# Linear attention and MLP on one core: k and v by casting software loads in nine rows per partition, with a block-diagonal k

## The chip, the cores and the metric

The kernel runs on 1 core of one Trainium2 chip. The metric is the device time of one execution in microseconds (us), lower is better. A change counts as faster or slower from 2% on; below that it is "same". TensorE is called PE, its weight load PEld, VectorE DVE, ScalarE ACT, GpSimd POOL, SyncE SP, as in the profile.

## The reference

For each of 8 batches and 8 heads (576 positions, 64 columns each), k and v are contracted over the positions, q is multiplied by the 64 x 64 result, each row is normalized by its root mean square and scaled; all heads side by side are the input of an MLP with a sigmoid gate.

```python
kv  = einsum('bhsd,bhse->bhde', k, v)            # 8 x 8 heads, s = 576, d = e = 64
out = einsum('bhsd,bhde->bhse', q, kv)
x   = out / sqrt(mean(out * out, -1) + 1e-6) * g_norm      # -> 4608 x 512
h   = x @ w_in                                    # 512 x 2048
y   = (h * sigmoid(1.702 * h)) @ w_out            # 2048 x 512
```

## The kernel before

The program has nine MLP stages (t = 0 to 8). While PE does the MLP of batch t, the attention of batch t + 1 is woven in at fixed step numbers: "fo" counts the 16 column blocks of the first MLP half (`units1`), n counts the 64 matmuls of the second (`units2`). Stage 8 does the last 64 rows of all batches together and has no attention.

The parts that the change touches:

```python
def load_batch(b, queue=nc.sync):                 # plain f32 loads, 512 of the 576 positions
    for n in "qkv":
        queue.dma_start(out=t, in_=srcs[n][b, :, 0:SM, :].rearrange("h (p j) d -> p h (j d)", j=J))   # J = 4
        # ... (rest rows of q)
    for n in "kv":                                # the other 64 positions: "rest rows"
        queue.dma_start(out=t, in_=srcs[n][b, :, SM:S, :].rearrange("h p d -> p h d"))

def casts(b):                                     # f32 -> f16: VectorE for q, k, v, GpSimd for the rest rows
    # ... 12 tensor_copy on VectorE, 3 on GpSimd

def kv(self, c):                                  # one head pair
    for j in range(J):
        nc.tensor.matmul(t[:, c, :].rearrange("p (l d) -> p l d", l=2), kh[:, c, j, :],
                         vh[:, 2 * c : 2 * c + 2, j * D : (j + 1) * D], start=(j == 0), stop=False)
    nc.tensor.matmul(t[:, c, :], kr[:, c, :], vr[:, c, :], start=False, stop=True)    # rest rows
    if c == NPAIR - 1:
        self.keep_kv()                            # only the two diagonal 64 x 64 blocks are kept
```

Each kv matmul has both heads of a pair in its 128 weight columns and both heads' v in its 128 moving columns, so half of what it computes (head 0 with head 1) is thrown away. Batch 0 has its own start-up path, and batch 1 (`Second`) a third layout, 96 partitions of six rows.

Of the kernel before, what the change touches and what calls it, by code (L numbers as in the profile page):

```python
# [7 lines left out]
F16 = mybir.dt.float16  # L8
# [8 lines left out]
def kernel(  # L17
# [28 lines left out]
    GROUP = 6  # L46
    assert PE_ * NJ == S and PE_ % 32 == 0

    const = ctx.enter_context(tc.tile_pool(name="const", bufs=1))
# [14 lines left out]
    kvb = [const.tile([P, NPAIR, P], F16, name=f"kvb{i}") for i in range(2)]  # L64
    krem = [const.tile([P, NPAIR, P], F16, name=f"krem{i}") for i in range(2)]
    vrem = [const.tile([P, NPAIR, P], F16, name=f"vrem{i}") for i in range(2)]
    qrem = [const.tile([P, 2, P], F16, name=f"qrem{i}") for i in range(2)]
# [26 lines left out]
    def pack(n, dst, c):  # L94

        nc.vector.tensor_copy(
            out=dst[0:PE_, c * NJ * P : (c + 1) * NJ * P].rearrange(
                "p (j l d) -> p j l d", j=NJ, l=2
            ),
            in_=raw[n][0:PE_, c, :].rearrange("p (l j d) -> p j l d", l=2, j=NJ),  # L100
        )


    kh = kbuf[:, 0 : NPAIR * SM].rearrange("p (c j e) -> p c j e", c=NPAIR, j=J)
    qh = qbuf[:, 0 : NPAIR * SM].rearrange("p (c j e) -> p c j e", c=NPAIR, j=J)
    vh = vbuf.rearrange("p c x -> p (c x)")[:, 0 : NPAIR * SM].rearrange("p (h x) -> p h x", h=H)

    def load_batch(b, queue=nc.sync):
        tiles = {}
        for n in "qkv":  # L110
            t = tiles[n] = stage.tile([P, H, J * D], F32, name=f"{n}f", tag=f"{n}f")
            queue.dma_start(
                out=t, in_=srcs[n][b, :, 0:SM, :].rearrange("h (p j) d -> p h (j d)", j=J)
            )
            if n == "q":
                t = tiles["qr"] = stage.tile([P, 4, D], F32, name="qrf", tag="qrf")
                for g in range(2):
                    queue.dma_start(
                        out=t[g * R : (g + 1) * R],
                        in_=q[b, 4 * g : 4 * g + 4, SM:S, :].rearrange("h p d -> p h d"),  # L120
                    )
        for n in "kv":
            t = tiles[n + "r"] = stage.tile([R, H, D], F32, name=f"{n}rf", tag=f"{n}rf")
            queue.dma_start(out=t, in_=srcs[n][b, :, SM:S, :].rearrange("h p d -> p h d"))
        staged[b] = tiles

    def casts(b):
        src = staged[b]
        for n, dst in (("q", qh), ("k", kh), ("v", vh)):
            for c in range(NPAIR):  # L130
                h = slice(2 * c, 2 * c + 2)
                if n == "v":
                    nc.vector.tensor_copy(out=vh[:, h, :], in_=src["v"][:, h, :])  # L133
                else:
                    nc.vector.tensor_copy(
                        out=dst[:, c, :, :].rearrange("p j (l d) -> p j l d", l=2),
                        in_=src[n][:, h, :].rearrange("p l (j d) -> p j l d", j=J),
                    )
        for n, t in (("kr", krem[b % 2][0:R]), ("vr", vrem[b % 2][0:R]), ("qr", qrem[b % 2])):
            nc.gpsimd.tensor_copy(out=t.rearrange("p c (l d) -> p (c l) d", l=2), in_=src[n])  # L140

# [60 lines left out]
    class Attention:  # L202
        ss_pool = (ps_a, "att")

        def __init__(self, b):
# [5 lines left out]
            else:  # L211
                self.x = x.rearrange("p (m r) -> p m r", r=P)
                xT[b] = x.rearrange("p (j c r) -> p c j r", j=J, c=KO)
                self.x16 = attn.tile([P, J, DM], F16, name="x16", tag="x16", bufs=1)

        def kv(self, c):
            if c == 0:
                self.kvp = ps_a.tile([P, NPAIR, P], F32, name="kvp", tag="att")
            t = self.kvp
            for j in range(J):  # L220
                nc.tensor.matmul(  # L221
                    t[:, c, :].rearrange("p (l d) -> p l d", l=2),
                    kh[:, c, j, :],
                    vh[:, 2 * c : 2 * c + 2, j * D : (j + 1) * D],
                    start=(j == 0),
                    stop=False,
                )
            kr, vr = krem[self.b % 2], vrem[self.b % 2]
            nc.tensor.matmul(t[:, c, :], kr[:, c, :], vr[:, c, :], start=False, stop=True)  # L229
            if c == NPAIR - 1:  # L230
                self.keep_kv()

        def keep_kv(self, c0=0, c1=NPAIR):
            for hl in range(2):
                r = slice(hl * D, (hl + 1) * D)
                nc.vector.tensor_copy(self.kb[r, c0:c1, r], self.kvp[r, c0:c1, r])  # L236

# [163 lines left out]
    class Second(Attention):  # L401
# [4 lines left out]
        def pack_q(self, c):  # L406
            pack("q", qbuf, c)

        def pack_k(self, c):
            pack("k", kbuf, c)  # L410

        def kv(self, c):
            if c % 2 == 0:
                self.kvp = ps_a.tile([P, NPAIR, P], F32, name="kvp", tag="att")
            t = self.kvp
            v2 = vbuf[0:PE_, c, :].rearrange("p (l x) -> p l x", l=2)
            for j in range(NJ):
                nc.tensor.matmul(  # L418
                    t[:, c, :].rearrange("p (l d) -> p l d", l=2),
                    kbuf[0:PE_, (c * NJ + j) * P : (c * NJ + j + 1) * P],  # L420
                    v2[:, :, j * D : (j + 1) * D],
                    start=(j == 0),
                    stop=(j == NJ - 1),
                )
            if c % 2:
                self.keep_kv(c - 1, c + 1)

# [201 lines left out]
    for c in (0, 2):  # L629
        early_load("k", 1, c, c + 2)  # L630
        early_load("v", 1, c, c + 2)
        load_w_out(8 + 2 * c, 12 + 2 * c)
    load_batch(2, nc.gpsimd)

# [7 lines left out]
    for t in range(NT):  # L642
# [3 lines left out]
        def at1(i, f, *args):  # L646
            u1.setdefault(i, []).append(lambda: f(*args))
# [7 lines left out]
        if t == 0:  # L655
# [4 lines left out]
            at1(8, start, 1)  # L660
            for r in krem + vrem:
                at1(8, nc.vector.memset, r[R:P], 0.0)
            for c in range(NPAIR):
                at1(12, of(1, "pack_q", c))
                at2(9 + 3 * c, of(1, "q", c))
                at2((21, 21, 33, 33)[c], of(1, "pack_k", c))
                at2((23, 24, 42, 43)[c], of(1, "kv", c))
                o = (27, 31, 48, 52)[c]
                at2(o, of(1, "out", c))
                at2(o + 7 - c // 2, of(1, "ss", c))  # L670
                at2(o + 7 - c // 2, of(1, "apply", c))
        elif b < B:
# [5 lines left out]
            f0 = 5 if t == 1 else 2  # L678
            at1(f0, casts, b)
            at1(f0, start, b)  # L680
            at1(f0, of(b, "transpose_q"))
            if t + 2 < B:
                at1(f0, load_batch, t + 2)
            for c in range(NPAIR):
                at1((10 if t == 1 else 9) + c, of(b, "kv", c))
            at2(6, nc.scalar.preload_act_table_set, "natural_log_exp_and_others")
# [38 lines left out]
```

## Time and profile before

| | before |
|---|---|
| time, median of 3 | 288.6 us (288.12 to 288.72) |
| profiled span | 286.0 us |
| PE busy | 279.8 us, 98% |
| VectorE busy | 110.9 us, 39% |
| a steady stage | 29.90 us, PE busy in all of it |
| DMA busy | 90% or more from 7 to about 57 us, then in bursts |

How to read it: PE is the bound, not only by its busy share but because the chain of work that ended last is PE work end to end. What PE does not execute and does not wait for cannot move the time. The prediction shows the lines.

### The profile page before, as it was taken

Reading aid. Unit: us, or ns where it says so; the run is one execution under the profiler, and the core shown is the slowest. Engines: PE = TensorE matmul, PEld = TensorE weight load, DVE = VectorE, ACT = ScalarE, POOL = GpSimd, SP = SyncE. Lnnn points to the kernel's source line nnn. Section 1 sums busy time; section 2 is a strip of 40 time slices with the busy share of each in tenths; the row PEclk is TensorE's granted clock in tenths of the full one; section 3 lists DMA queues with packets and bytes.
Section 4 is the critical chain, followed back from the end, with each engine's and each line's share of the span. In section 5 each row is a group of like instructions: output and inputs, shape, how many; then the busy total and the mean of one; then the engine's idle time right before and its main releaser. Section 6 shows DMA issues by size and latency. Waiting matters only on the chain.

```text
span 286.0 us, 4103 instructions
## 1 busy us (share of the span) xinstructions
PE 279.8 (98%) x1609; PEld 136.0 (48%) x1609; DVE 110.9 (39%) x219; ACT 156.1 (55%) x273; POOL 49.2 (17%) x66
## 2 busy tenths in 40 slices
PE   7899999999999999999999999999999999999994
PEld 3444544455445544554455445544554444444444
DVE  3530544627651656147603860386227400110001
ACT  2697358766575645574468536763666375017400
POOL 8831430201400140014000500032002100000000
PEclk9999999999999999999999999999999999999999
DMA  8999999999679537893699358954601230011022
GB/s 179 203 206 204 204 255 320 256 250 311 147 178 331 134 75 220 233 271 58 201 205 323 57 183 202 323 92 127 139 2 37 53 133 0 0 73 76 0 73 73
DMA packets 63589, 45.82 MB, mean 160 GB/s; under 512 B 36195, under 2 KB 60515, under 8 KB 62803
## 3 DMA queue, kind: packets, MB, share of 16 engines
q1 hardware_dynamic: 53344, 33.74, 45.4%
q0 software_dynamic: 9504, 10.86, 19.9%
q10 hardware_dynamic: 722, 0.97, 1.2%
q8 instruction: 12, 0.20, 0.3%
q14 instruction: 7, 0.05, 0.1%
HBM read 36.73 MB, written 9.44 MB: 161 GB/s over the span
## 4 chain that ended last, share of the span: by engine, by line
PE 94%; DMA 2%; POOL 2%; issue 0%; DVE 0%; POOLq 0%
PE hT L453 44%; PE o L490 42%; DMA vbuf<-in_v_dram 2%; PE kvp L221 2%; PE outR L287 2%; PE oh L520 1%; PE ss L335 1%; POOL qraw L89 1%; POOL kraw L89 1%; PE outT L255 1%; PE kvp L418 0%; PE kvp L229 0%; POOL vbuf L89 0%; PE q L431 0%; PE outT L266 0%
## 5 line engine op out<-in xcount | busy, mean ns | idle before, releaser
L490 PE MATMUL o<-w_out_sb,gT 128*128 128x512 f16 x560 | 130.7, 379 | 0.0
L462 ACT ACTIVATE gT<-hT 128x512 f16<-128x512 f32 x144 | 84.5, 599 | 77.3 <-PE hT L453 77.2
L453 PE MATMUL hT<-xT,w_in_sb 128*128 128x512 f16 x512 | 116.4, 379 | 0.0
L453 PEld LDWEIGHTS <-w_in_sb 128*128 128x128 f16 x576 | 54.9, 98 | 62.9 <-DMA w_in_sb<-in_moe_w_in_dram 1.6
L490 PEld LDWEIGHTS <-gT 128*128 128x128 f16 x560 | 53.0, 98 | 56.3 <-issue 0.2
L319 POOL TENSOR_TENSOR x<-xr,g_all 128x512 f16<-128x512 f32 x12 | 15.2, 1270 | 141.3 <-DMA vf<-in_v_dram 67.0
L500 DVE COPY osb<-o 128x512 f32<-128x512 f32 x20 | 13.8, 691 | 63.5 <-PE o L490 63.5
L298 DVE TENSOR_REDUCE sum<-sq 128x8 f32<-128x512 f16 x24 | 15.8, 678 | 18.3 <-ACT sq L295 18.3
L236 DVE CAST kvb<-kvp 64x256 f16<-64x256 f32 (+1 forms) x16 | 6.2, 388 | 43.1 <-PE kvp L229 42.0
L312 DVE TENSOR_TENSOR xr<-outR,sum 128x512 f32<-128x512 f32 x24 | 15.5, 686 | 11.1 <-ACT sum L309 11.1
L319 DVE TENSOR_TENSOR x<-xr,g_all 128x512 f16<-128x512 f32 x12 | 15.2, 1267 | 0.7
L295 ACT ACTIVATE sq<-outR 128x512 f16<-128x512 f32 x24 | 13.6, 590 | 2.0 <-PE outR L287 1.6
L275 ACT ACTIVATE sq<-outT 128x512 f16<-128x512 f32 (+1 forms) x16 | 7.7, 482 | 11.9 <-PE outT L255 10.5
L453 PE MATMUL hT<-x_rem,w_in_sb 128*128 128x512 f16 x64 | 14.0, 379 | 0.0
L500 ACT COPY osb<-o 128x512 f32<-128x512 f32 x15 | 8.7, 580 | 6.3 <-PE o L490 6.3
L308 ACT ACTIVATE sum<-sum,eps_t 128x16 f32<-128x16 f32 x12 | 3.7, 308 | 15.0 <-DVE sum L298 14.9
L337 ACT ACTIVATE ln<-ss,eps_t 128x512 f32<-128x512 f32 (+1 forms) x16 | 9.3, 584 | 2.9 <-PE ss L335 2.7
L133 DVE CAST vbuf<-vf 128x512 f16<-128x512 f32 x24 | 9.6, 459 | 2.0 <-DMA vf<-in_v_dram 2.0
L462 ACT ACT_TABLE_LOAD x8 | 10.3, 1283 | 0.1
L221 PEld LDWEIGHTS <-kbuf 128*128 128x128 f16 x96 | 7.4, 98 | 5.7
L287 PEld LDWEIGHTS <-qTd 128*128 128x128 f16 x96 | 7.4, 98 | 5.7
L221 PE MATMUL kvp<-vbuf,kbuf 128*128 128x128 f16 x96 | 9.3, 219 | 0.0
(73 smaller groups left out, 156.8 us busy)
## 6 DMA issues: line engine op xcount, KB each, us to landing
out_dram<-osb SPq DMA_DIRECT2D x6, 1024.0 KB, 4.3
qf<-in_q_dram SPq DMA_DIRECT2D x5, 1024.0 KB, 5.8
kf<-in_k_dram SPq DMA_DIRECT2D x5, 1024.0 KB, 7.8
vf<-in_v_dram SPq DMA_DIRECT2D x5, 1024.0 KB, 10.5
w_out_sb<-in_moe_w_out_dram POOLq DMA_DIRECT2D x4, 512.0 KB, 17.2
out_dram<-osb SPq DMA_DIRECT2D x6, 192.0 KB, 4.2
qf<-in_q_dram POOLq DMA_DIRECT2D x1, 1024.0 KB, 16.7
kf<-in_k_dram POOLq DMA_DIRECT2D x1, 1024.0 KB, 14.8
```

Of the source, the lines that this page charges most:

```text
L133: nc.vector.tensor_copy(out=vh[:, h, :], in_=src["v"][:, h, :])
L221: nc.tensor.matmul(t[:, c, :].rearrange("p (l d) -> p l d", l=2), kh[:, c, j, :], vh[:, 2 * c : 2 * c + 2, j * D : (j + 1) * D], start=(j ...
L287: nc.tensor.matmul(t[:, c * P : (c + 1) * P], self.qT[c][:, j * P : (j + 1) * P], self.kb[:, c, :], start=True, stop=True,)
L295: nc.scalar.activation(sq, t, AFT.Square)
L298: nc.vector.tensor_reduce(out=self.sum2[:, j % 2, :], in_=sq.rearrange("p (h d) -> p h d", h=H), op=ALU.add, axis=mybir.AxisListType.X,)
L312: nc.vector.tensor_mul(xr[:, i], self.o[j + i].rearrange("p (h d) -> p h d", h=H), s2[:, i, :].unsqueeze(2).to_broadcast([P, H, D]),)
L319: (nc.vector if i else nc.gpsimd).tensor_mul(self.x16[:, j + i, :].rearrange("p (h d) -> p h d", h=H), xr[:, i], g_all.unsqueeze(1).to_bro ...
L337: nc.scalar.activation(ln[:, 0:n], t[:, 0:n], AFT.Ln, bias=eps_t, scale=1.0 / D)
L453: nc.tensor.matmul(self.h[fo], w_in_sb[:, ko, fo * P : (fo + 1) * P], self.x[:, ko], start=(ko == 0), stop=(ko == KO - 1),)
L462: nc.scalar.activation(self.gT[:, fo, :], self.h[fo], AFT.Gelu_apprx_sigmoid)
L490: nc.tensor.matmul(os[mo], gT[:, fo, mo * P : (mo + 1) * P], w_out_sb[:, fo, :], start=(fo == 0), stop=(fo == FO - 1),)
L500: copy(osb[:, mo, :], os[mo])
```

## The change

The intent: let the DMA cast k and v on the way in (f32 to f16), so that the f32 staging and the eight casts per batch go; take nine rows per partition in 64 partitions, so that 576 = 64 x 9 comes out even and no rest rows are left; and put the two heads of a pair into the two halves of the partitions. The k of a pair is then made block-diagonal (head 0 in partitions 0 to 63 and columns 0 to 63, head 1 in the rest, zeros elsewhere), so that one matmul of 64 columns does both heads and computes nothing that is thrown away. The same path now serves batch 1.

```diff
-    krem, vrem = ...                                # rest rows
+    kpad = const.tile([P, NPAIR, NH, P], F16)       # block-diagonal k, NH = 9
+    def load_half(n, b, c0, c1):
+        for l in range(2):
+            nc.gpsimd.dma_start(
+                out=raw[n][l * PH : (l + 1) * PH, c0:c1, 0 : NH * D],
+                in_=srcs[n][b].rearrange("(c l) (p j) d -> l p c (j d)", l=2, j=NH)[l][:, c0:c1],
+            )
+        def pack_k(self, c):
+            for l in range(2):
+                r = slice(l * PH, (l + 1) * PH)
+                nc.vector.tensor_copy(
+                    out=kpad[r, c, :, l * D : (l + 1) * D],
+                    in_=kraw[r, c, 0 : NH * D].rearrange("p (j d) -> p j d", j=NH),
+                )
         def kv(self, c):
-            ...                                     # 4 + 1 matmuls of 128 columns
+            for j in range(NH):                     # 9 matmuls of 64 columns
+                nc.tensor.matmul(self.kvp[:, c, :], kpad[:, c, j, :], vbuf[:, c, j * D : (j + 1) * D],
+                                 start=(j == 0), stop=(j == NH - 1))
# ... batch 1, in the second half of stage 0:
-                at2((23, 24, 42, 43)[c], of(1, "kv", c))
-                o = (27, 31, 48, 52)[c]
+                at2((25, 27, 42, 43)[c], of(1, "kv", c))
+                o = (31, 34, 50, 53)[c]
# ... sums and applies of batch 1 at 38, 46, 56, 59 in place of 34, 38, 54, 58
# ... steady stages: k and v of batch t + 2 asked for at fo = 13 (14 in stage 1), after the last kv matmul of batch t + 1
+                at1((10 if t == 1 else 9) + 4, load_kv, t + 2)
```

More of the change, by code (lines that the diff above doesn't have):

```diff
@@ L47 @@
     assert PE_ * NJ == S and PE_ % 32 == 0
+    PH = P // 2
+    NH = S // PH
+    assert PH == D and PH * NH == S
     const = ctx.enter_context(tc.tile_pool(name="const", bufs=1))
@@ L64 @@
     kvb = [const.tile([P, NPAIR, P], F16, name=f"kvb{i}") for i in range(2)]
-    krem = [const.tile([P, NPAIR, P], F16, name=f"krem{i}") for i in range(2)]
-    vrem = [const.tile([P, NPAIR, P], F16, name=f"vrem{i}") for i in range(2)]
+    kpad = const.tile([P, NPAIR, NH, P], F16)
     qrem = [const.tile([P, 2, P], F16, name=f"qrem{i}") for i in range(2)]
@@ L101, in pack @@
         )
-    kh = kbuf[:, 0 : NPAIR * SM].rearrange("p (c j e) -> p c j e", c=NPAIR, j=J)
     qh = qbuf[:, 0 : NPAIR * SM].rearrange("p (c j e) -> p c j e", c=NPAIR, j=J)
-    vh = vbuf.rearrange("p c x -> p (c x)")[:, 0 : NPAIR * SM].rearrange("p (h x) -> p h x", h=H)
-    def load_batch(b, queue=nc.sync):
-        tiles = {}
-        for n in "qkv":
-            t = tiles[n] = stage.tile([P, H, J * D], F32, name=f"{n}f", tag=f"{n}f")
+    def load_half(n, b, c0, c1):
[4 more added lines that the diff above has]
+            )
@@ L112, in load_batch, with load_kv, load_q @@
+    def load_kv(b):
+        load_half("k", b, 0, NPAIR)
+        load_half("v", b, 0, NPAIR)
+    def load_q(b, queue=nc.sync):
+        t = stage.tile([P, H, J * D], F32, name="qf", tag="qf")
+        queue.dma_start(out=t, in_=q[b, :, 0:SM, :].rearrange("h (p j) d -> p h (j d)", j=J))
+        r = stage.tile([P, 4, D], F32, name="qrf", tag="qrf")
+        for g in range(2):
             queue.dma_start(
-                out=t, in_=srcs[n][b, :, 0:SM, :].rearrange("h (p j) d -> p h (j d)", j=J)
-            )
@@ L115, in load_batch @@
-            if n == "q":
-                t = tiles["qr"] = stage.tile([P, 4, D], F32, name="qrf", tag="qrf")
-                for g in range(2):
-                    queue.dma_start(
-                        out=t[g * R : (g + 1) * R],
-                        in_=q[b, 4 * g : 4 * g + 4, SM:S, :].rearrange("h p d -> p h d"),
-                    )
-        for n in "kv":
-            t = tiles[n + "r"] = stage.tile([R, H, D], F32, name=f"{n}rf", tag=f"{n}rf")
-            queue.dma_start(out=t, in_=srcs[n][b, :, SM:S, :].rearrange("h p d -> p h d"))
@@ L125, in load_batch @@
-        staged[b] = tiles
-    def casts(b):
-        src = staged[b]
-        for n, dst in (("q", qh), ("k", kh), ("v", vh)):
-            for c in range(NPAIR):
-                h = slice(2 * c, 2 * c + 2)
-                if n == "v":
-                    nc.vector.tensor_copy(out=vh[:, h, :], in_=src["v"][:, h, :])
-                else:
-                    nc.vector.tensor_copy(
-                        out=dst[:, c, :, :].rearrange("p j (l d) -> p j l d", l=2),
-                        in_=src[n][:, h, :].rearrange("p l (j d) -> p j l d", j=J),
-                    )
-        for n, t in (("kr", krem[b % 2][0:R]), ("vr", vrem[b % 2][0:R]), ("qr", qrem[b % 2])):
-            nc.gpsimd.tensor_copy(out=t.rearrange("p c (l d) -> p (c l) d", l=2), in_=src[n])
+                out=r[g * R : (g + 1) * R],
@@ new lines, in load_q, with cast_q @@
+                in_=q[b, 4 * g : 4 * g + 4, SM:S, :].rearrange("h p d -> p h d"),
+            )
+        staged[b] = (t, r)
+    def cast_q(b):
+        t, r = staged[b]
+        nc.gpsimd.tensor_copy(out=qrem[b % 2].rearrange("p c (l d) -> p (c l) d", l=2), in_=r)
+        for c in range(NPAIR):
+            nc.vector.tensor_copy(
+                out=qh[:, c, :, :].rearrange("p j (l d) -> p j l d", l=2),
+                in_=t[:, 2 * c : 2 * c + 2, :].rearrange("p l (j d) -> p j l d", j=J),
+            )
@@ L214, in __init__ @@
                 self.x16 = attn.tile([P, J, DM], F16, name="x16", tag="x16", bufs=1)
+        def pack_k(self, c):
+            for l in range(2):
+                r = slice(l * PH, (l + 1) * PH)
+                nc.vector.tensor_copy(
+                    out=kpad[r, c, :, l * D : (l + 1) * D],
+                    in_=kraw[r, c, 0 : NH * D].rearrange("p (j d) -> p j d", j=NH),
+                )
         def kv(self, c):
-            if c == 0:
-                self.kvp = ps_a.tile([P, NPAIR, P], F32, name="kvp", tag="att")
-            t = self.kvp
-            for j in range(J):
+            if c % 2 == 0:
+                self.kvp = ps_a.tile([P, NPAIR, D], F32, name="kvp", tag="att")
+            for j in range(NH):
                 nc.tensor.matmul(
-                    t[:, c, :].rearrange("p (l d) -> p l d", l=2),
-                    kh[:, c, j, :],
-                    vh[:, 2 * c : 2 * c + 2, j * D : (j + 1) * D],
+                    self.kvp[:, c, :],
+                    kpad[:, c, j, :],
+                    vbuf[:, c, j * D : (j + 1) * D],
                     start=(j == 0),
-                    stop=False,
+                    stop=(j == NH - 1),
                 )
-            kr, vr = krem[self.b % 2], vrem[self.b % 2]
-            nc.tensor.matmul(t[:, c, :], kr[:, c, :], vr[:, c, :], start=False, stop=True)
-            if c == NPAIR - 1:
-                self.keep_kv()
+            if c % 2:
+                self.keep_kv(c - 1, c + 1)
         def keep_kv(self, c0=0, c1=NPAIR):
@@ L235, in keep_kv @@
                 r = slice(hl * D, (hl + 1) * D)
-                nc.vector.tensor_copy(self.kb[r, c0:c1, r], self.kvp[r, c0:c1, r])
+                nc.vector.tensor_copy(self.kb[r, c0:c1, r], self.kvp[r, c0:c1, :])
         def transpose_q(self):
@@ L407, in pack_q @@
             pack("q", qbuf, c)
-        def pack_k(self, c):
-            pack("k", kbuf, c)
-        def kv(self, c):
-            if c % 2 == 0:
-                self.kvp = ps_a.tile([P, NPAIR, P], F32, name="kvp", tag="att")
-            t = self.kvp
-            v2 = vbuf[0:PE_, c, :].rearrange("p (l x) -> p l x", l=2)
-            for j in range(NJ):
-                nc.tensor.matmul(
-                    t[:, c, :].rearrange("p (l d) -> p l d", l=2),
-                    kbuf[0:PE_, (c * NJ + j) * P : (c * NJ + j + 1) * P],
-                    v2[:, :, j * D : (j + 1) * D],
-                    start=(j == 0),
-                    stop=(j == NJ - 1),
-                )
-            if c % 2:
-                self.keep_kv(c - 1, c + 1)
         def q(self, c):
@@ L629 @@
     for c in (0, 2):
-        early_load("k", 1, c, c + 2)
-        early_load("v", 1, c, c + 2)
+        load_half("k", 1, c, c + 2)
+        load_half("v", 1, c, c + 2)
         load_w_out(8 + 2 * c, 12 + 2 * c)
-    load_batch(2, nc.gpsimd)
+    load_q(2, nc.gpsimd)
     nc.gpsimd.dma_start(out=g_all, in_=g_norm.unsqueeze(0).to_broadcast([P, D]))
@@ L660 @@
             at1(8, start, 1)
-            for r in krem + vrem:
-                at1(8, nc.vector.memset, r[R:P], 0.0)
+            for l in range(2):
+                r = slice(l * PH, (l + 1) * PH)
+                at1(8, nc.vector.memset, kpad[r, :, :, (1 - l) * D : (2 - l) * D], 0.0)
             for c in range(NPAIR):
@@ L666 @@
                 at2((21, 21, 33, 33)[c], of(1, "pack_k", c))
-                at2((23, 24, 42, 43)[c], of(1, "kv", c))
-                o = (27, 31, 48, 52)[c]
+                at2((25, 27, 42, 43)[c], of(1, "kv", c))
+                o = (31, 34, 50, 53)[c]
                 at2(o, of(1, "out", c))
-                at2(o + 7 - c // 2, of(1, "ss", c))
-                at2(o + 7 - c // 2, of(1, "apply", c))
+                if c == NPAIR - 1:
+                    at2(46, load_kv, 2)
+                at2((38, 46, 56, 59)[c], of(1, "ss", c))
+                at2((38, 46, 56, 59)[c], of(1, "apply", c))
         elif b < B:
@@ L678 @@
             f0 = 5 if t == 1 else 2
-            at1(f0, casts, b)
+            at1(f0, cast_q, b)
             at1(f0, start, b)
@@ L682 @@
             if t + 2 < B:
-                at1(f0, load_batch, t + 2)
+                at1(f0, load_q, t + 2)
+                at1((10 if t == 1 else 9) + 4, load_kv, t + 2)
             for c in range(NPAIR):
+                at1(f0, of(b, "pack_k", c))
                 at1((10 if t == 1 else 9) + c, of(b, "kv", c))
```

## The prediction

> **What bounds the kernel now.** I read the page first, for busy time by engine.
>
> ```profile
> PE 279.8 (98%) x1609; PEld 136.0 (48%) x1609; DVE 110.9 (39%) x219; ACT 156.1 (55%) x273; POOL 49.2 (17%) x66
> ```
>
> TensorE (PE) is busy for 98% of the 286.0 us span; VectorE, which the change relieves, for 39%. A busy share is only an average, so I read PE's own waits next, then PE busy time by stretch (columns: stretch, its length, busy time of PE, PEld, DVE, ACT and POOL with instruction counts, granted clock, DMA share, GB/s).
>
> ```profile
> PE idle L569 <- DVE kvb L156: 1.3, 1, 1.3
> PE kv L372 <- DMA vbuf<-in_v_dram: 0.6, 1, 0.6
> PE q L389 <- ACT qraw L560: 0.3, 1, 0.3
> ...
> 29.00:47.30 18.30, 18.26 (x122) 9.28 (x121) 8.75 (x21) 9.64 (x16) 5.95 (x8) 1.00 1.20 247
> 47.30:77.40 30.10, 30.10 (x176) 14.88 (x175) 16.67 (x30) 20.47 (x38) 6.39 (x8) 1.00 0.99 252
> 77.40:107.30 29.90, 29.90 (x171) 14.76 (x170) 14.30 (x27) 17.58 (x32) 4.46 (x5) 1.00 0.70 181
> ```
>
> PE waits 2.2 us in the whole run, all in batch 0's start-up, which the diff leaves alone. After that every stretch is full: 29.90 of 29.90 us in a steady stage, at full clock. So only two things can move the time: fewer PE columns in a changed place, or a new PE wait.
>
> A busy PE could still hide slack, so the third view is the chain of work that ended last, within the third stage (start, length, work):
>
> ```profile
> 86.17 0.22 PE kvp L221 x4
> 86.39 0.06 PE kvp L229
> 86.45 0.86 PE hT L453 x4
> ...
> 99.40 0.12 PE outT L266 x4
> 99.52 1.94 PE o L490 x9
> ```
>
> It is PE work end to end. It also gives the unit costs: a 128-column matmul spaces at 0.28 / 5 = 56 ns, rest rows (L229) included; a 512-column one at 0.86 / 4 = 216 ns; a 64-column one (outT L266) at 0.12 / 4 = 30 ns, each with a fresh weight load.
>
> Last, the issues of software loads on POOL and what they wait for, because the first 57 us are where DMA is full and the change reorders them.
>
> ```profile
> 26.53 0.75 POOL L194 DMA_DIRECT2D w_out_sb<-in_moe_w_out_dram  x1 [2.08 <-DMA w_out_sb<-in_moe_w_out_dram]
> 34.71 0.95 POOL L112 DMA_DIRECT2D kf<-in_k_dram  x1 [0.86 <-DMA vbuf<-in_v_dram]
> 37.52 0.89 POOL L112 DMA_DIRECT2D vf<-in_v_dram  x1 [1.87 <-DMA w_out_sb<-in_moe_w_out_dram]
> 38.69 0.69 POOL L124 DMA_DIRECT2D krf<-in_k_dram  x1 [0.28 <-DMA kraw<-in_k_dram]
> 40.16 0.69 POOL L124 DMA_DIRECT2D vrf<-in_v_dram  x1 [0.77 <-DMA vbuf<-in_v_dram]
> 42.74 0.57 POOL L635 DMA_DIRECT2D g_all<-in_g_norm_dram  x1 [1.90 <-DMA w_out_sb<-in_moe_w_out_dram]
> ```
>
> Counting back in the list of issues, each of these starts as the transfer eight issues earlier lands: in this kernel eight software loads are outstanding at most. The releases therefore date the landings: batch 1's second k at 38.4 us or just after, its second v at 40.1, the last w_out at 42.7.
>
> [...]
>
> **The change, part by part.**
>
> *PE.* Per head pair and batch, six batches with rest rows go from 4 + 1 matmuls of 128 columns, 5 x 56 = 280 ns, to nine of 64, 9 x 30 = 270 ns[...]. Only the diagonal blocks are computed now, so 640 columns become 576[...]. [...] Batch 1 goes from six matmuls of 128 columns (0.34 us for L418 x6 in the chain) to nine of 64: 0.07 x 4 = 0.28 us. All of it is on the path. One caution: nine matmuls in a row now add into the same 64 columns. The nearest thing in the trace is batch 0's kv (L372), twelve accumulating 64-column matmuls in 0.39 us, 32.5 ns each. With that spacing the six batches lose 0.0125 x 24 = 0.3 us and batch 1 gains 0.19. So PE moves between -0.6 and +0.1 us; I take -0.45.
>
> *VectorE.* Gone per steady batch: four k casts (418 ns) and four v casts (459 ns mean), 3.5 us. Added: eight copies of 64 x 576 f16. Batch 1's pack of 96 x 768 f16 took 350 ns for k; with some 60 ns fixed (the smallest VectorE instructions take 59) that is 0.38 ns an element, so an estimated 280 ns, and 8 x 280 = 2.2 us. The kvb evacuation becomes four of 64 x 128 (286 ns) for two of 64 x 256 (422), +0.3 us. Net -1 us a batch on an engine busy 14.3 of 29.9: worth nothing, off the path.
>
> *POOL.* Gone: the k and v rest casts, 1.0 + 0.64 us a batch. Added: four issues of about 0.7 us. A wash, far from the bound.
>
> *DMA.* HBM reads stay equal: 512 + 64 rows before, 576 after. SBUF writes halve, 1 KB and 256 B rows become 2304 B ones, and k and v leave the SP queue where they stood behind the q transposes. In a steady stage v is asked for after the last kv matmul, at fo=13, and is used at fo=9 of the next stage, some 26 us later; before, the whole batch landed within about 11 us of issue. Hidden by a wide margin.
>
> *First stage.* Batch 1's k and v become eight loads, kv of the first half moves two or three steps later, the sums later too, and batch 2's k and v go last, from about 40 us. By POOL's list with eight outstanding, the queue always holds several transfers of 0.3 to 1 MB, so it does not run dry. The margins, as estimates: kv of batch 1's second half sits at step 42, 40.99 us before; one sums matmul (0.22 us) and 0.14 of kv saving now precede it less, so it comes near 40.6, against v at 40.1: 0.5 us. Its k, landed at 38.4, needs 4 x 0.28 = 1.1 us of copies, to 39.5. Batch 2's v: from 42.7 to its landing near 54.5 the same bytes queue as before (q, k, v and the first output), so it lands near 54.5 again, and kv of batch 2 now needs no v cast and runs at about 56.4: 2 us of margin, where before the last v cast ended at 56.88 with kv starting at 56.78.
>
> Sum: 288.6 - 0.45 = 288.15, plus an expected 0.15 for a chance of a first-stage wait: 288.3.
>
> **The rivals.** *A: a new wait in the first stage.* For it: DMA is full until 57 us[...], and the margin at step 42 is 0.5 us. Batch 1's k and v are 2.36 MB; if they ran 20% slower than the roughly 410 GB/s read rate, they would land 1.2 us later and PE would stall about 0.7 us (288.9)[...]. [...] *B: PE spacing.* If a matmul with a full weight load into the same 64 columns spaced at 56 ns rather than 30, each pair would cost 0.50 us for 0.28: 24 x 0.22 + 4 x 0.16 = 6 us, 294.5. Against it are L266 at 30 and L372 at 32.5. *C: relief of VectorE and DMA brings a gain of several us.* This is what the intent suggests, but no wait of PE on either is there to remove after 14 us; the chain has none. I give it almost nothing. *D: software loads starved in steady stages.* The 26 us of room covers it; the time would stay.
>
> **Range and chances.** The best case is -0.6 us with the 0.3 us of scatter between runs: 287.4. The upper end takes A at a moderate size: 289.8. Faster by over 2% would be under 282.8, for which no mechanism exists: 0.01. Slower by over 2% is over 294.4, which needs B or an extreme A: 0.04.
>
> **What would show it.** Right: nine kv matmuls in about 0.27 us in the chain, a steady stage of 29.86 us or so, full PE stretches after 14 us, copies of 0.28 us into the block-diagonal k, no PE wait on the k copies or v loads. Wrong: a PE or PEld wait on the v buffer or the k copy near 35, 41 or 56 us (A), or a kv group of 0.5 us (B), or a steady stage shorter by more than 0.1 us (C).

The sum came to 288.3 us: 288.6 - 0.45 + 0.15. Terms under its -0.45 are cut: by the measured spacing, which stands, kv in the six batches saves 280 - 270 = 10 ns a pair, 0.24 us in all, and with batch 1's 0.28 us that is 0.52; a cut term took the saving somewhat higher, and the best case of -0.6 us comes from there. The 410 GB/s of rival A is twice the 206 GB/s that the trace before shows from 12 to 28 us, counted as written, which is half of what a cast from f32 to f16 reads.

## The result

| | before | after |
|---|---|---|
| time, median | 288.66 us (288.12 to 289.06, 4 runs) | 287.88 us (287.74 to 287.90, 4 runs) |
| ratio, 95% interval | | 0.9973 (0.9956 to 0.9990) |
| profiled span | 286.0 us | 285.6 us |
| last PE work ends (below) | 282.35 us | 281.66 us |
| VectorE busy | 110.9 us | 119.3 us |

A ratio is the mean time of one kernel's fast runs over that of the other's of the same rounds, so not quite the ratio of the medians. The change saves 0.27%, 0.8 us by the medians. By the 2% measure that is "same", and 287.88 lies in the range of 287.4 to 289.8.

The page after, busy time by engine:

```profile
PE 278.9 (98%) x1717; PEld 135.4 (47%) x1717; DVE 119.3 (42%) x233; ACT 156.1 (55%) x273; POOL 56.0 (20%) x78
```

PE has 108 matmuls more (252 of 64 columns for 144 of 128) and is busy for 0.9 us less. VectorE did not get less to do but 8.4 us more.

The same stretches after (columns as in the prediction):

```profile
29.00:47.09 18.09, 17.89 (x133) 8.84 (x132) 10.07 (x25) 9.53 (x16) 7.72 (x12) 1.00 1.20 231
47.09:77.23 30.14, 30.14 (x191) 14.89 (x190) 17.05 (x32) 20.57 (x38) 6.19 (x8) 1.00 0.91 187
77.23:107.06 29.83, 29.83 (x187) 14.65 (x185) 15.42 (x29) 17.45 (x32) 5.83 (x7) 1.00 0.68 140
```

The steady stage went from 29.90 to 29.83 us and is still full. The stretch that starts at 29 us is no longer quite full: PE is idle for 0.20 us of it, where before it was 0.04.

Busy time hides short waits, since one matmul starts before the one ahead of it has ended (512 columns: 379 ns long, 216 apart); the spacing of PE's starts shows them. By it the kernel before lost time in this stretch too: 0.20 us at 36.81 us, 0.08 at 39.92 and 0.14 at 43.10, so 0.41 in all. The first and the last are waits for the copies of kv's result out of PSUM (kvb), as PE's weight loads show (waited for: us in total, times, longest):

```profile
PEld L255 <- DVE kvb L236: 1.0, 2, 0.5
```

The chain after, the kv groups of the third stage:

```profile
85.87 0.26 PE kvp L227 x9
86.13 0.86 PE hT L438 x4
```

Nine matmuls of 64 columns take 0.26 us, 29 ns each, where five of 128 took 0.28. And the end of PE's work, before and then after (start, length):

```profile
278.84 3.51 PE oh L520 x32
```

```profile
278.15 3.51 PE oh L505 x32
```

PE ends 0.69 us earlier. By stage borders, 0.29 us of it is won by the end of the first stage (47.38 to 47.09), 0.01 in the second and 0.06 to 0.13 in each of the next five. Of the 0.29, 0.12 were there already when the second half of the first stage began (28.74 to 28.62 us), before anything new is used; e1, the same kernel again, begins it at 29.03, so these 0.12 are within its scatter.

What is new among the waits, in the first stage: PE's weight loads wait for the copies into the block-diagonal k. The second line is the group of these copies, the last the copies of batch 1's first half in order of time.

```profile
PEld L227 <- DVE kpad L218: 0.9, 2, 0.6
```

```profile
L218 DVE COPY kpad<-kraw 64x576 f16<-64x576 f16 x56 | 25.0, 446 | 2.0 <-DMA kraw<-in_k_dram 0.7
```

```profile
34.44 1.87 DVE L218 COPY kpad<-kraw 64x576 f16<-64x576 f16 x4
```

A copy takes 446 ns, not the 280 of the prediction. So the four of the first half end at 36.3 us and not at 35.6, and the second kv group starts 0.26 us late: after its two MLP matmuls, at 35.68 + 2 x 0.216 = 36.11 us, it was free to go, and it started at 36.37.

The chain after also names a second place, the last load of w_out (slices 12 to 15):

```profile
33.04 9.53 DMA w_out_sb<-in_moe_w_out_dram
42.57 0.04 issue
42.61 0.81 PE o L475 x3
```

It lands at 42.57 us, and PE stands at step 48, the first that needs these slices: four matmuls took 1.29 us in place of 1.03. PE, being a little earlier, met a transfer that it had not met before. The two new waits cost 0.26 us each, 0.52 together; the 0.41 us of old ones are gone from their places, so waits in this stage grew by 0.11 us net.

### The profile page after: what moved, and what is told of

It is laid out like the page before. It is cut to its first block, busy times and chain, and to the rows that moved or that the text cites. A ratio compares the mean times of both kernels' runs of the same rounds, so it can differ in the third digit from the quotient of the medians.

```text
span 285.6 us, 4343 instructions
## 1 busy us (share of the span) xinstructions
PE 278.9 (98%) x1717; PEld 135.4 (47%) x1717; DVE 119.3 (42%) x233; ACT 156.1 (55%) x273; POOL 56.0 (20%) x78
## 4 chain that ended last, share of the span: by engine, by line
PE 85%; DMA 11%; ACT 1%; POOL 1%; DVE 0%; issue 0%
PE o L475 39%; PE hT L438 39%; DMA w_out_sb<-in_moe_w_out_dram 10%; PE kvp L227 2%; PE outR L291 2%; DMA qf<-in_q_dram 2%; PE oh L505 1%; PE ss L339 1%; PE idle L554 0%; PE q L393 0%; POOL vbuf L112 0%; PE outT L259 0%; ACT qraw L545 0%; PE outT L270 0%; POOL qraw L91 0%
## 5 line engine op out<-in xcount | busy, mean ns | idle before, releaser
L438 PEld LDWEIGHTS <-w_in_sb 128*128 128x128 f16 x576 | 54.5, 98 | 62.3 <-DMA w_in_sb<-in_moe_w_in_dram 0.5
L218 DVE COPY kpad<-kraw 64x576 f16<-64x576 f16 x56 | 25.0, 446 | 2.0 <-DMA kraw<-in_k_dram 0.7
L240 DVE CAST kvb<-kvp 64x128 f16<-64x128 f32 x28 | 8.1, 288 | 36.5 <-PE kvp L227 36.3
L112 POOL DMA_DIRECT2D kraw<-in_k_dram x16 | 9.9, 624 | 49.4 <-DVE kpad L218 43.5
L112 POOL DMA_DIRECT2D vbuf<-in_v_dram x16 | 9.7, 608 | 34.0 <-PE kvp L227 29.3
L227 PEld LDWEIGHTS <-kpad 128*128 128x128 f16 x252 | 11.0, 98 | 7.0 <-DVE kpad L218 0.9
L227 PE MATMUL kvp<-vbuf,kpad 128*128 128x64 f16 x252 | 11.9, 193 | 0.1
```

The source lines that it names most:

```text
L112: nc.gpsimd.dma_start(out=raw[n][l * PH : (l + 1) * PH, c0:c1, 0 : NH * D], in_=srcs[n][b].rearrange("(c l) (p j) d -> l p c (j d)", l=2, ...
L218: nc.vector.tensor_copy(out=kpad[r, c, :, l * D : (l + 1) * D], in_=kraw[r, c, 0 : NH * D].rearrange("p (j d) -> p j d", j=NH),)
L227: nc.tensor.matmul(self.kvp[:, c, :], kpad[:, c, j, :], vbuf[:, c, j * D : (j + 1) * D], start=(j == 0), stop=(j == NH - 1),)
L438: nc.tensor.matmul(self.h[fo], w_in_sb[:, ko, fo * P : (fo + 1) * P], self.x[:, ko], start=(ko == 0), stop=(ko == KO - 1),)
```

## The experiments

All kernels gave right results. Where an expectation gave a reason that no run here shows, the reason is cut and the cut marked (in e8 and e11); the figures that e8 expected stand, those for e11's loads went with their reason. Each line of a diff is against the changed kernel. The kernel before ran and its median was 288.37 to 288.55 us.

### e1: the changed kernel again

No edit.

> The changed kernel, unedited. Theory (PE columns alone set the time): 287.9 us, 0.7 us under the kernel before, since 0.56 to 0.6 us of PE columns went away; the steady stage again 29.82 to 29.84 us for 29.90 of before. It also shows what varies from run to run: PE weight loads waited 0.5 us for w_in here and 1.6 us before, and that loads are not touched by the change, so I expect between 0.4 and 1.7 us, at random. Rival (the reordering of loads gives part of the gain): the w_in waits stay near 0.5 us in this second profile and the gain is over 0.8 us.

Measured: 287.93 us (287.86 to 288.10), ratio 0.9976 (0.9963 to 0.9988). The gain repeats. The w_in wait, which was 0.5 us in the first profile of the changed kernel, is this time as in the profile before:

```profile
PEld L438 <- DMA w_in_sb<-in_moe_w_in_dram: 1.6, 4, 0.5
```

In the other runs below it lies between nothing and 1.6 us. It varies from run to run and is not the change's doing. With it the w_out wait comes and goes: when the head of the run is slower, PE reaches step 48 after the transfer has landed, and in this profile the four matmuls took 1.07 us.

### e2: half of batch 1's copies to ScalarE

```diff
-                nc.vector.tensor_copy(
+                copy = nc.scalar.copy if self.b == 1 and l else nc.vector.tensor_copy
+                copy(
                     out=kpad[r, c, :, l * D : (l + 1) * D],
```

> Batch 1's copies into the block-diagonal k: the lower half goes to ScalarE, so that the first pair is ready some 0.45 us sooner. Theory 1 (the last w_out slice, landing at 42.6 us, holds PE at step 48 of the first stage and gives back what is won before it): the wait of PE weight loads on the copy, 0.9 us in two places of which about 0.3 us costs PE time, goes away, but PE then waits up to 0.3 us longer for w_out, and the time stays within 0.15 us of e1_again. Theory 2 (the copy wait is on the path by itself): 0.3 us faster than e1_again.

Measured: 287.80 us (287.36 to 288.01), ratio 0.9966 (0.9954 to 0.9979). The second kv group now starts at 36.01 us, without a wait. But the wait for w_out grew, as theory 1 has it; it now shows on PE itself:

```profile
42.54 0.81 PE L476 MATMUL o<-w_out_sb,gT 128*128 128x512 f16 x3 [0.40 <-DMA w_out_sb<-in_moe_w_out_dram]
```

The matmul before it started at 41.76, so this one is 0.56 us late. Won at 36 us, given back at 42. The 0.13 us between the medians of e1 and e2 is within the scatter.

### e3: the last load of w_out in two

```diff
-        load_w_out(8 + 2 * c, 12 + 2 * c)
+        for f in range(8 + 2 * c, 12 + 2 * c, 2 if c else 4):
+            load_w_out(f, f + (2 if c else 4))
```

> The last w_out load of four slices is cut into two of two, so the slices that step 48 needs first land about 1.3 us earlier. Theory 1 (PE waits about 0.26 us for w_out at step 48): that wait goes, and the time is 0.2 to 0.3 us under e1_again. Theory 2 (that gap in the trace has another cause, or is caught up by a later wait): within 0.1 us of e1_again.

Measured: 287.77 us (287.49 to 287.92), ratio 0.9970 (0.9956 to 0.9983). The wait is gone: step 48's four matmuls take 0.86 us from 42.33 (in the chain, where the next start ends them). It is gone narrowly: the second of the two loads landed at 42.76 us, and PE used it from 42.81. The profile falls out as theory 1 says; the time, 0.16 us under e1, leans that way but does not settle it, and since the wait depends on the head of each run it could not be more than 0.26 us on average.

### e4: both of these, and whole loads

e2 and e3, and the two half loads as one over 128 partitions, which works because the two heads of a pair follow each other in memory:

```diff
-        for l in range(2):
-            nc.gpsimd.dma_start(out=raw[n][l * PH : (l + 1) * PH, c0:c1, 0 : NH * D], in_=...)
+        nc.gpsimd.dma_start(
+            out=raw[n][:, c0:c1, 0 : NH * D],
+            in_=srcs[n][b].rearrange("(c l) (p j) d -> (l p) c (j d)", l=2, j=NH)[:, c0:c1],
+        )
```

> All three together: k and v each as one load over 128 partitions (the two heads of a pair lie one behind the other, so both halves are one pattern), ScalarE for half of batch 1's copies, w_out's last load in two. Theory 1: copy wait and w_out wait both gone, 0.4 to 0.6 us under e1_again, about 287.4. Rival: the time stays at e1_again, because a third wait (the sums and applies of batch 1 at the border to the second stage) takes their place.

Measured: 287.54 us (287.45 to 287.69), ratio 0.9961 (0.9949 to 0.9974). Its slowest run is faster than the fastest of e1, so it beats both kernels, by 0.4 us and 1.0 us. Neither the copy wait nor the w_out wait is in its trace. But PE, earlier once more, meets the copy of kv's result, as the rival had it in kind: the matmul behind step 50 starts 0.15 us late (0.38 us in the chain, for its own 0.22).

```profile
43.24 0.38 PE outT L259
```

So of the 0.52 us of the two new waits about 0.4 is won.

### e5: kv with twice the columns

```diff
-                    vbuf[:, c, j * D : (j + 1) * D],
+                    vbuf[:, c, j * D : (j + 1) * D].unsqueeze(1).to_broadcast([P, 2, D]),
```

The target in PSUM becomes 128 wide; the second copy of the columns is not used.

> The same kernel, but each kv matmul streams its 64 columns of v twice, 128 columns for 64 (the second copy is not used, the result stays right). Nothing else changes. Theory (kv's PE columns are on the path, one for one): 9 x (56 - 29) = 0.24 us a pair, 28 pairs, 6.8 us slower than the changed kernel, about 294.7 us; a steady stage of 30.8 us. Rival (PE has slack at these places, or the weight load and not the columns sets the spacing of 64-column matmuls): much less, 0 to 3 us.

Measured: 294.28 us (293.90 to 294.38), 6.4 us over the changed kernel, ratio 1.0194 to the one before (1.0180 to 1.0208, "unclear" by the 2% measure, but clear of 1). In the chain:

```profile
87.58 0.50 PE kvp L227 x9
88.09 0.86 PE hT L438 x4
```

0.50 for 0.26 us, 28 times: 6.7 us of PE work, and 6.4 of them arrive in the time. PE columns in kv are on the path nearly one for one. It also shows the spacing of a 128-column matmul with a fresh 128 x 128 weight load, 56 ns, and of a 64-column one, 29: the columns set it and the weight load does not.

### e6: twice the copies on VectorE

```diff
+                if self.b > 1:
+                    nc.vector.tensor_copy(out=kjunk[r, :, l * D : (l + 1) * D], in_=...)   # the same again
```

> Every copy into the block-diagonal k of batches 2 to 7 is done twice, the second into a buffer nobody reads: 8 x 0.45 = 3.6 us more VectorE work in each of six stages, 21 us in all, double of what the copies cost. Theory (VectorE is off the path, so neither its relief nor its load moves the time): within 0.3 us of the changed kernel. Rival (relief of VectorE was worth something): slower by 1 us or more, with PE waiting on k copies or on casts of q.

Measured: 287.83 us (287.52 to 288.13), ratio 0.9973 (0.9959 to 0.9987), against 0.9973 of the changed kernel.

```profile
PE 278.6 (98%) x1717; PEld 135.5 (47%) x1717; DVE 136.9 (48%) x281; ACT 156.0 (55%) x273; POOL 55.8 (20%) x78
```

VectorE has 17.6 us more than in the changed kernel and nothing happens. In steady stages its relief would be worth nothing either.

### e7: k and v asked for later

```diff
-                at1((10 if t == 1 else 9) + 4, load_kv, t + 2)
+                at2(48, load_kv, t + 2)
```

> k and v of batches 3 to 7 are asked for 48 steps into the second half of a stage in place of fo=13 of the first, some 13 us later, so 11 us before kv needs them instead of some 26. Theory (loads hidden by a wide margin, landing about 6 us after issue): same time within 0.3 us, though the copies into k now wait on their load. Rival (software loads need the room): PE weight loads wait for the k copy or v in each stage, 1 us or more a stage, 5 us or more in all.

Measured: 334.28 us (333.19 to 334.54), ratio 1.1586 (1.1568 to 1.1603). The expectation missed by 46 us, and the rival's 5 us too. Four full stages took 38.2 to 39.8 us each. PE does not wait for k or v:

```profile
PE hT L438 <- DMA xT<-x: 34.2, 5, 7.3
```

It waits for the transposing DMA that turns the normalized x for the next stage. The next two fences give its time from issue to landing, in the stretch from 71 to 86 us: first the changed kernel, then e7.

```profile
xT<-x SPq DMA_TRANSPOSE x1, 3.1
```

```profile
xT<-x SPq DMA_TRANSPOSE x1, 10.3
```

GpSimd, which has nothing to wait for at this place, issues the loads from 72.6 us on; the transpose is issued at 73.3, and PE wants its result at 77.2. Alone it would land 0.8 us early. Beside the software loads it landed at 83.6. The waits are 34 of the 46 us. In the stages where PE stood still the granted clock was lower too (0.91 from 77 to 154 us), and most of the rest is the slower pace after each wait: the first eleven matmuls took 4.55 us, some 0.41 each, where 512 columns otherwise space at 0.22. That is 11 x (0.41 - 0.22) = 2.1 us for this wait; an estimate from it is some 10 us for the five.

```profile
83.66 4.55 PE L438 MATMUL hT<-xT,w_in_sb 128*128 128x512 f16 x11 [6.35 <-DMA xT<-x]
```

### e8: whole loads alone

The third edit of e4 alone.

> Each pair of half loads (64 partitions each) becomes one load over all 128 partitions with the same bytes and rows. Theory [...]: the last w_out slice lands within 0.3 us of before, time within 0.2 us of the changed kernel. Rival [...]: the loads land 1 us or more earlier, the wait for w_out goes, and the time falls by 0.3 us.

Measured: 287.77 us (287.67 to 287.99), ratio 0.9972 (0.9960 to 0.9985). The same as the changed kernel, and the last w_out slice landed at 42.52 us, for 42.57 in the changed kernel: two halves of 64 partitions are no slower than one load of 128 here.

### e9: late, but behind the transpose of x

```diff
+    def gate_x(b):                                  # GpSimd reads two columns of the transposed x
+        nc.gpsimd.tensor_copy(out=xjunk, in_=live[b].x[:, NPAIR * J - 1, 0:2])
...
+                at2(48, gate_x, b)
                 at2(48, load_kv, t + 2)
```

> e7_late_loads cost 46 us, against what was expected of it; its trace has PE waiting 34 us for the transposing DMA of x, which took 10.3 us instead of 3.1 beside the software loads. Here the loads sit at the same late place, but GpSimd first reads two columns of the transposed x, so the loads start only when that transpose has landed (near 76.6 us in the second stage). They then have even less time before kv, some 9 us. Theory (the loads hurt only because they run beside the transpose of x, which has under 1 us to spare): the wait on x is gone, steady stages at 29.8 to 31.5 us, 288 to 297 us in all, the rest of the loss being waits of kv for v. Rival (the loads were simply too late for kv, or software loads starve any transposing DMA): 320 us or more, or the wait moves in full to the transpose of q.

Measured: 318.3 us (317.76 to 319.28), ratio 1.1033. The wait for x is gone, and its transpose lands in 2.8 us again (median of 12). So the loads beside it were what held it. But the time came out 21 us above the range of the theory, because a load that starts this late is too late for kv:

```profile
PE kvp L231 <- DMA vbuf<-in_v_dram: 21.5, 5, 5.3
```

PE waits for v in five stages and for the copy of k in some (PEld waited 6.1 us for it). v took 10.8 us to land (median), not 6: it now ran beside k and beside the transpose of q, which this time had the room. The rival is half right: late loads lose either way, first by the transpose, then by themselves. The wait did not move to the transpose of q. How the DMA engines share between a transposing DMA and software loads stays open. That the loads slow the transpose is shown; that the transpose slows the loads is not separated here from k and v running side by side.

### e10: batch 1 at its old steps

```diff
-                at2((25, 27, 42, 43)[c], of(1, "kv", c))
-                o = (31, 34, 50, 53)[c]
+                at2((23, 24, 42, 43)[c], of(1, "kv", c))
+                o = (27, 31, 48, 52)[c]
# sums and applies at o + 7 - c // 2 again
```

> Batch 1's kv, out and sums back at the step numbers of the kernel before; all else as changed. The copies into the block-diagonal k take 0.45 us each, not the 0.28 us of the estimate, so the first pair is ready at 35.4 us and the second at 36.3, while steps 23 and 24 come near 34.9 and 35.4. Theory: PE waits on the copies about 0.5 and 0.6 us, and the time is 0.3 to 0.8 us above the changed kernel, 288.2 to 288.7. Rival (the w_out slice catches everything up at step 48 anyway): within 0.2 us of the changed kernel.

Measured: 288.98 us (288.61 to 289.11), ratio 1.0012 (0.9998 to 1.0027), 1.1 us over the changed kernel: more than expected. Without the moved steps the change would have gained nothing. Two of its waits in the first stage:

```profile
PEld L227 <- DVE kpad L218: 1.4, 2, 0.8
...
PEld L259 <- DVE kvb L240: 1.2, 2, 0.6
```

The late copies held kv, kv held the copy of its result (kvb), and that held the matmul with q. The chain of this run goes through four copies in a row, 34.83 to 36.62 us, and later through the logarithms and exponentials of the sums. The w_out load did not absorb it, because PE was by then later than the transfer.

### e11: copies and loads by themselves

Extra copies and loads in stages 7 and 8, on buffers that are free by then.

```diff
+        for _ in range(3):
+            nc.vector.tensor_copy(out=kpad[0:PH, 0, :, 0:D], in_=src[0:PH])             # L131: as the kernel has it
+        # L133 at partition 64; L135 no gaps; L137 eight rows; L139 128 partitions;
+        # L141 128 partitions, eight rows; L143 128 partitions, no gaps
+        # loads: half of k; k over 128 partitions; both halves
```

> The changed kernel with extra copies and loads in its last two stages, where VectorE and the DMA are nearly idle; their results are not used. Copies of f16, three of each: 64 x 576 into every other 64 columns as the kernel has it, at partition 0 and at 64; 64 x 576 without gaps; 64 x 512 and 128 x 512 with gaps; 128 x 576 with and without gaps. Idea A (nine rows of 64 are an odd outer count[...]): 512 takes far less than 576 with gaps, and 576 without gaps is fast. Idea B (64 partitions or the start at 64 cost): 128 partitions faster. Idea C (gaps cost): both with gaps slow. Loads alone: one half of k over 64 partitions, then the whole k and v pattern over 128 partitions, then both halves one behind the other. [...]

Measured: 287.5 us, one run. The copies by shape (busy time, mean ns of one; six of each):

```profile
L139 DVE COPY kjunk<-kraw 128x576 f16<-128x576 f16 x6 | 2.7, 453 | 0.2
L133 DVE COPY kpad<-kraw 64x576 f16<-64x576 f16 x6 | 2.7, 449 | 0.2
L131 DVE COPY kpad<-kraw 64x576 f16<-64x576 f16 x6 | 2.6, 441 | 0.1
L143 DVE COPY kjunk<-kraw 128x576 f16<-128x576 f16 x6 | 1.9, 310 | 0.2
L135 DVE COPY kjunk<-kraw 64x576 f16<-64x576 f16 x6 | 1.8, 302 | 0.2
L141 DVE COPY kjunk<-kraw 128x512 f16<-128x512 f16 x6 | 1.8, 294 | 0.2
L137 DVE COPY kjunk<-kraw 64x512 f16<-64x512 f16 x6 | 1.7, 285 | 0.2
```

The number of partitions does not matter (453 and 441, 294 and 285), nor does the start at partition 64 (449). Gaps alone do not (285 with gaps for 512). Nine rows with gaps cost 446, eight 285, and 576 without gaps 302. So idea A: the outer count of nine.

The run's trace file keeps the access patterns as they were encoded, and there nine is the count of the destination alone: the rows of the source touch and were merged into one run of 576. Eight rows are encoded as 512 into 8 x 64. A copy with nine gapped rows on both sides was not run, so whether the nine by itself or its meeting one run of 576 makes it slow is not shown.

The fast copies of the traces lie on one line: 285 ns for 512 elements, 302 for 576, 350 for 768 (batch 1's k, kernel before), 453 for 1152 (e12). From these, an estimate of some 150 ns fixed and 0.26 ns an element; the nine-row copy comes to (446 - 150) / 576 = 0.51, about double.

The loads did not come out as planned: the half that was to run alone had to wait for the copies, and ran just ahead of the whole one. But the whole load and the two halves can still be compared, by the rates in the stretch from 238 to 247 us (40 slices of 0.225 us, GB/s as written). The first half landed at 240.68 us, so the whole load is alone from slice 12 to 22; the two halves of the right part ran one after the other (landed at 245.67 and 247.12), so a half is alone there at the end:

```profile
GB/s 92 36 36 36 220 195 215 200 215 190 215 200 215 205 205 215 205 220 195 225 195 200 77 15 51 67 123 225 189 225 205 200 179 236 200 210 210 149 46 0
```

All run at about 205 GB/s.

### e12: two head pairs in one copy

e3 and e8, and:

```diff
+            if c % 2:
+                return
-                    out=kpad[r, c, :, l * D : (l + 1) * D],
+                    out=kpad[r, c : c + 2, :, l * D : (l + 1) * D],
```

> Whole loads and the split w_out load as in e4, but the copies stay on VectorE and take two head pairs at once: 64 x 1152, an even outer count of two, four copies a batch in place of eight. From e11 (with gaps 446 ns for nine rows, 285 for eight, 302 for 576 without gaps) some 0.42 ns an element above 59 ns fixed: about 545 ns a copy, 2.2 us a batch for 3.6 (idea A: the outer count of nine made the copies slow). If it is not the outer count, about 830 ns. Batch 1's first two pairs are then ready at 34.4 + 1.1 = 35.5 us for kv at 35.4 and 36.1, so PE waits 0.1 us at most on the copies. Time: as e4_whole_act_split, ratio to the kernel before 0.996 (0.9950 to 0.9970); VectorE's 9 us of relief in steady stages gives nothing more.

Measured: 287.49 us median (287.30 to 288.22), ratio 0.9972 (0.9958 to 0.9985).

```profile
L219 DVE COPY kpad<-kraw 64x1152 f16<-64x1152 f16 x28 | 12.7, 453 | 1.9 <-DMA kraw<-in_k_dram 1.5
```

Twice the elements in the time of one copy before, 453 ns for 446: idea A holds (as encoded, 2 x 576 into 18 x 64), and more than expected (545, which took 59 ns as the fixed part). VectorE has 107.1 us in all, 12.2 less than in the changed kernel, and PE's weight loads wait 0.4 us on the copies for 0.9. The time is not told apart from the changed kernel's: one run in five was slow by 0.7 us, and the ratio is that of e8. What e4 has, a copy wait of nothing, is not quite reached here, and the split w_out load is met after all: its second half landed at 42.74 us and PE was ready 0.18 us earlier. Of the versions tried, e4 is the one that is shown to be faster.

## Why the prediction was right, and where its steps were not

**The bound and the direction were right.** PE sets the time, and what is added to PE's work comes out in the time (e5: 6.7 us of work in, 6.4 us out). The unit costs from the trace before held: 0.26 us a kv group against 0.27 predicted, a steady stage of 29.83 us against 29.86.

**The PE step was too small.** The caution about nine matmuls into the same 64 columns, 32.5 ns each, did not come true. From start to next start, the 24 kv groups of batches 2 to 7 went from 6.70 to 6.28 us and the four of batch 1 from 1.34 to 1.07: 0.70 us where 0.45 was taken. Measured were -0.69 us to the end of PE's work and about -0.8 in the medians. That 0.69 meets 0.70 is partly luck: the waits of the first stage grew by 0.11 us, and its head was 0.12 us faster in this profile.

**"After that every stretch is full" was not quite so.** The prediction read PE's own waits and busy time; PE's weight loads and the spacing of starts show 0.41 us of waits in batch 1's part of the first stage. The 0.15 us that it allowed for a new wait there is close to the net 0.11, but as a chance balance of 0.52 us of new waits against 0.41 of old ones that it did not know of.

**The VectorE step was wrong in size and sign.** It forecast 1 us a batch less; the steady stage shown has 15.42 us of VectorE for 14.30, so 1.1 more. "An estimated 280 ns" took 60 ns as the fixed part, and the estimate in e11 gives 150, so 302 for a fast copy; and nine gapped rows are not a fast copy, but 446 ns (e11, e12). The casts that went were also cheaper than "3.5 us", a sum of means: one starts before the one ahead has ended, and eight of them are busy for 3.0 us ((9.6 + 8.5) / 6, before):

```profile
L133 DVE CAST vbuf<-vf 128x512 f16<-128x512 f32 x24 | 9.6, 459 | 2.0 <-DMA vf<-in_v_dram 2.0
L135 DVE CAST kbuf<-kf 128x512 f16<-128x512 f32 x24 | 8.5, 418 | 0.0
```

In all, 25.0 us of copies came, 18.1 of casts and 1.2 of batch 1's packing of k went, and 28 smaller evacuations of kv (+1.9) and larger zeroing (+1.0) come to it: about the 8.4 us measured. In steady stages this costs nothing, as the prediction argued for the opposite sign (e6). GpSimd, called a wash, has 56.0 us for 49.2, off the path as well.

**"No PE wait on the k copies" was wrong, by the same estimate.** In the first stage, where the copies do stand between a landing and PE, PE's weight loads waited for them, and PE lost 0.26 us at the second pair. The prediction put that margin at step 42 and on v; it was at step 27 and on the copy. Step 42 was met without a wait. At batch 2's v the 2 us of margin were less than 1: it landed at 55.74 us, not near 54.5, and kv began at 56.55.

**The moved steps were taken as neutral and are not.** They are worth 1.1 us (e10), which is more than the whole gain. The change wins 0.70 us of PE work, waits for its slower copies would take it back (by the spacing of starts, e10 loses 1.50 us in the first stage, the changed kernel 0.52), and the later steps hide most of them. What the later steps would bring to the kernel before, which has 0.41 us of waits there, was not tried, so how the gain divides between layout and schedule is shown only from this side.

**Rival A came, but small and by other causes.** Its sign, a wait on the k copy near 35 us, was seen at 36, from the copy's length. Neither k nor v was late; the last w_out slice was, since PE reached step 48 earlier. The prediction dated its landing at 42.7 us and did not ask who needs it. In e2, removing the copy wait leaves w_out to catch PE; e3, removing the other, gains too little to tell; removing both gains 0.4 us (e4). The worry about half loads was unfounded: e8 and e11 find no difference between halves and whole loads (last w_out slice at 42.52 us with whole loads, 42.57 with halves). In e11 the two halves ran one after the other, landing 1.45 us apart, and each ran at about 205 GB/s, as the whole load did.

**Rival B** (spacing by the weight load) is refuted by 29 ns. **Rival C** (a gain of several us by relief of VectorE and DMA) is refuted by e6 and by the result.

**Rival D was dismissed rightly, but for the wrong reason.** The loads are hidden where the change put them. But "the 26 us of room covers it" counted only the time until kv. The room ends earlier, where x is transposed for the next stage: the loads have to be through by then (e7), and starting them after it is too late (e9). The change's place, just behind the last kv matmul, falls between the two transposes; only the one of x was shown to matter.

## What to carry to other kernels

When an engine is full end to end, price a change in that engine's own units and look for new waits only where the data comes just in time; here 0.70 us of columns was all there was to win, and a few waits of 0.1 to 0.3 us in the first stage decided how much of it stayed. Look for such waits in the spacing of starts; a busy share of 100% can hide them (before, 18.26 us busy of 18.30 hid 0.41 us of waits). The room of a transfer ends not at its own use but at the first transfer it slows that someone is waiting for (e7: the transpose of x took 10.3 us beside the loads, 3.1 without). An estimate for a copy needs a measured copy of the same shape on both sides, not only of the same element count, and a fixed part taken from copies (here 446 ns where 280 was estimated).
